# Second transform stages and inverse as 32x32 tiles of the TensorE array

## The chip, the cores and the metric

The kernel runs on one NeuronCore of one Trainium2 chip; the other cores are idle. The metric is the device time of one execution in microseconds (us). The engines are called by their names in the profile: PE (TensorE: matmuls, and PEld, its weight loads), DVE (VectorE), ACT (ScalarE), POOL (GpSimd) and SP (SyncE, used here to issue DMAs). A matmul multiplies a stationary operand (lhsT, loaded as weights) with a moving one (rhs, up to 512 columns) and writes PSUM, which has 8 banks of 512 fp32 columns in each of 128 partitions.

## What is computed

With x = A_q (2048 rows, 512 channels), all in bf16:

```python
xn = layernorm(x)                                  # over the channels
# branch A: a causal shift filter of 4 taps, then a long convolution over the 2048 rows
k_shift[s] = sum over t of k_pad[s + t] * shift_k[3 - t]
kv = k_shift * v
y  = irfft(rfft(kv, 4096) * rfft(ssm_k, 4096))[:2048] + kv * ssm_D
s  = xn * y
# branch B: a gated feed-forward, 512 -> 1792 -> 512
h = gelu(xn @ w_gate) * (xn @ w_up)
g = silu(h @ w_down)
out = x + s * g
```

## The kernel before

**The feed-forward** goes in four quarters of 512 rows. For each quarter, `unit(q, m)` (m = 0 to 13) makes 128 hidden columns: four gate and four up matmuls, a Gelu on ACT (L1149) and a product on DVE (L1152). `down(q)` multiplies back. These matmuls take most of PE's time and need one PSUM bank at a time each (`pF`, at most four banks).

**The long convolution** is a Fourier transform in two stages, done as matmuls, once for the filter ("H", with ssm_D folded in as its first sample) and once for kv ("K"):

- `stage1` (16 tiles of rows each) multiplies with the tables F1, copies the pair of banks out on ACT, and stores to a scratch tensor in HBM (ZH or ZK) whose layout does the reordering between the stages. There are 32 groups of 128 rows in this layout.
- The second stage multiplies each group with `MT[:, 0, :]`, a 128x128 matrix that MSK has made block-diagonal: four blocks of 32x32 on its diagonal, zeros elsewhere. For H, `h_stage2(n)` (n = 0 to 15) does a pair of groups: load BH from ZH, two matmuls (`fwd`), copy out on ACT, store to ZS.
- The spectrum loop at L1063 (n = 0 to 15) does a pair of K groups each: load BK from ZK, two matmuls, multiply with the spectrum HS (two arrays, loaded from ZS by two DMAs, over even and odd partitions), invert, copy out on ACT (BO), store to ZI. The real and imaginary parts lie in even and odd partitions, so the complex product is HB = K x HS[0] plus KS = (K with its even and odd partitions exchanged, and a sign) x HS[1].
- In 14 of the 16 rounds (`psum` true, set by N_SUM = 14) ACT copies K with a sign column (COLS[:, 2:3]) to KB, two DMAs exchange the partitions from KB to KS, DVE multiplies KS by HS[1] and adds it to HB, and the inverse is two matmuls with `MT[:, 1, :]`. In the other two rounds DVE makes KS from PSUM without an exchange, and the inverse adds two matmuls with `MT[:, 2, :]`, a second inverse matrix that contains the exchange.
- At the end BI is loaded from ZI, `y` multiplies with G1, the transposed F1 (32 matmuls), and DVE applies xn and the gate; results are stored as they come.

**The order of the work** on every engine is fixed when the program is built. `Sched` is a list scheduler: each task has an engine, an estimated duration, a priority (the P_... constants; lower goes first), buffers and predecessors; it emits the tasks in the order in which its model starts them. `Trk` puts in the semaphore waits that this order needs. So a task that comes late on the chip holds up what is behind it on its engine. PSUM is one pool of eight banks under two names: `pF` gives single banks from the top, `pC` pairs of banks from the bottom (at most NC_PAIRS = 3 pairs at a time) to the stages of the transform. The DMAs of a stage are issued on SP, those of ZH and ZI on ACT. All matmuls but the transposes are recorded under one line, L634, and all product instructions of the spectrum under L1084, so that groups are told apart by their tiles.

Of the kernel before, what the change touches and what calls it, by code (L numbers as in the profile page):

```python
# [14 lines left out]
DM = 512  # L15
# [13 lines left out]
NC_PAIRS = 3  # L29
SMALL = 1.15 * 262144  # L30
AHEAD = int(4.32)
N_SUM = int(14.8)
HS_FROM = int(13.29)
P_ZS = 0.01
P_HS = 0.2
P_BK = -1
P_KS = -0.49
P_XT = 0.25
P_G1 = 1.22
P_KB = 0.27  # L40
P_PI = 1
P_KM = 3.27
P_LN1 = 2.02
P_LN2 = 3.07
P_LN3 = 7.64
N_HOLD = 3

# [21 lines left out]
class Trk:  # L69
# [112 lines left out]
    def op(self, key, fn, r=(), w=(), accum=False):  # L182
        E = self.engs[key]
        req = self._need(r, w, key, accum)
        with self.nc.body(E["body"]):
            self._do_waits(key, req)
            ins = fn(E["eng"])
            E["seq"] += 1
            v = E["seq"]
            ins.then_inc(E["sem"], 1)  # L190
        sname = E["sem"].name
        self.evid += 1
        snapd = dict(E["wm"])
        snapd[sname] = v
        self.snap[(sname, v)] = snapd
        self._record(r, w, (E["sem"], v, self.evid, key))
        return ins
# [24 lines left out]
class Pool_:  # L222
# [25 lines left out]

    def take(self, i):
        self.used += 1  # L250
        for j in range(i * self.size, (i + 1) * self.size):
            self.busy[j] = True
# [25 lines left out]
class Sched:  # L278


    SLACK = 214.66
# [3 lines left out]
    HEDGE = 1277.99  # L285
# [5 lines left out]
    QUEUE = {"ACT": 1887.67, "DVE": 7268.22}  # L291
    URGENT = 2.78
    DEFER = 11.14
# [49 lines left out]
    def run(self):  # L343
# [5 lines left out]
        while ready:  # L349
            cands = []  # L350
            for t in ready:
# [3 lines left out]
                ok = True  # L355
                for b in t.w:
                    if b.pool is not None and b.slot is None:
                        av = b.pool.find()
                        if av is None:
                            ok = False  # L360
                            break
                        base = max(base, av[0] + self.SEM)
# [60 lines left out]
def build_kernel(nc, A_q, A_k, A_v, A_shift_k, A_ssm_k, A_ssm_D, B_w_gate, B_w_up, B_w_down, out):  # L423
    with ExitStack() as es0:
# [61 lines left out]
        BH = at("BH", [128, 4, 2, DM], BF16, g_at + 8192)  # L486
# [3 lines left out]
        HS = new("HS", [128, 4, 2, 2, DM], BF16)  # L490
# [3 lines left out]
        BK = new("BK", [128, 4, 2, DM], BF16)  # L494
# [6 lines left out]
        ZS = nc.dram_tensor("ZS", [NG // 2, 128, 2, DM], BF16, kind="Internal")  # L501
# [45 lines left out]
        R_cols, R_col1, R_col2 = (res(f"COLS{i}", COLS[:, i:i + 1]) for i in range(3))  # L547
# [27 lines left out]
        R_BH = [res(f"BH{j}", BH[:, j, :, :]) for j in range(4)]  # L575
        R_BK = [res(f"BK{j}", BK[:, j, :, :]) for j in range(4)]
        R_HS = [twins(f"HS{j}", HS[:, j, :, :, :]) for j in range(4)]
        R_KB = [twins(f"KB{j}", KB[:, j, :, :]) for j in range(4)]
        R_KS = [twins(f"KS{j}", KS[:, j, :, :]) for j in range(4)]
# [17 lines left out]
        pBH = Pool_("BH", 4)  # L597
        pBK = Pool_("BK", 4)
        pKB = Pool_("KB", 4)
        pKS = Pool_("KS", 4)  # L600
        pHS = Pool_("HS", 4)
# [271 lines left out]
        def h_transpose(k):  # L873
# [12 lines left out]
            for hf in range(2):  # L886
                def ev(e, h, hf=hf):
# [3 lines left out]
                   rr=lambda hf=hf: R_bank(pp[hf]), ww=R_HTr[8 * hf:8 * hf + 8], prio=1))  # L891
# [20 lines left out]
        bsgn, bphi, bS32, bmsk, bm = B("sgn"), B("phi"), B("s32"), B("msk"), B("m16")  # L912
# [20 lines left out]
        small("DVE", 180.0, lambda h: h.tensor_scalar(COLS[:, 2:3], Q32[:, 10:11], -2.0, 1.0, ALU.mult, ALU.add), [q], [R_col2], [bq[10]], [bsgn])  # L933
# [42 lines left out]
        for t in range(NT):  # L976
            stage1("H", t, HTr[:, t, :], R_HTr[t], [bHTr[k][t // 8] for k in range(KD)], ZH, 1.51)
# [3 lines left out]
        skb = [op([("POOL", 950.0)], lambda e, h, j=j: h.tensor_copy(SKB[:, j, :], SKR[:].rearrange("p (d j) -> p j d", j=4)[:, j, :]), r=[bSKR], w=[bSKB[j]], rr=[R_SKR], ww=[R_SKB[j]], prio=3, after=xnT_tasks + mt_last) for j in (3, 2, 1, 0)]  # L981

        def kshift(i):
# [9 lines left out]
            def rkk(j):  # L993
# [8 lines left out]
               rr=lambda: rkk(3) + [R_SKB[3]], ww=lambda: [R_KAC[a.slot]], prio=4, **af)  # L1002
            for j in (2, 1, 0):
                m = B(f"ktm{i}_{j}", pKTM)
                op([("DVE", dur)], lambda e, h, j=j, m=m: h.tensor_tensor(KTM[:, m.slot, :, :], kk(j), sk(j), ALU.mult), r=need + [bSKB[j], a], w=[m],  # L1005
                   rr=lambda j=j: rkk(j) + [R_SKB[j]], ww=lambda m=m: [R_KTM[m.slot]], prio=4, after=mt_last + sin_tasks + skb)
                op([("DVE", dur)], lambda e, h, m=m: h.tensor_tensor(KAC[:, a.slot, :, :], KAC[:, a.slot, :, :], KTM[:, m.slot, :, :], ALU.add),  # L1007
                   r=[m], w=[a], rr=lambda m=m: [R_KTM[m.slot], R_KAC[a.slot]], ww=lambda: [R_KAC[a.slot]], prio=4)
            kshift_tasks.append(op([("DVE", dur)], lambda e, h: h.tensor_tensor(V[:, t0:t0 + 4, :], KAC[:, a.slot, :, :], V[:, t0:t0 + 4, :], ALU.mult),
               r=[a, bV[i]], w=[bKV[i]], rr=lambda: [R_KAC[a.slot]] + R_V[t0:t0 + 4], ww=R_V[t0:t0 + 4], prio=2.42))  # L1010
# [4 lines left out]
        def z_pair(Z, n):  # L1015
            return bass.AP(Z, 2 * n * 128 * DM, [[DM, 128], [128 * DM, 2], [1, DM]])

        def fwd(p, T, R_T, buf):
            def f(e):
                s = psl(p)  # L1020
                for i in range(2):
                    trk.op("PE", lambda h, i=i: mm(h, ps(s, i), MT[:, 0, :], T[:, buf.slot, i, :], True, True),
                           r=[*R_M, R_T[buf.slot]], w=[R_ps[s][i]], accum=True)
            return f

        d_bh = [dsem(f"d_bh{j}") for j in range(4)]
        h2_tasks = []

        def h_stage2(n):
            bh, p, a = B(f"bh{n}", pBH), B(f"psf{n}", pC), B(f"hf{n}", pAST["K"])  # L1030
            S.add([("SP", ISSUE)], lambda e, n=n, bh=bh: dma(e, BH[:, bh.slot, :, :], z_pair(ZH, n), d_bh[bh.slot], R_Z["H"], [R_BH[bh.slot]]),
                  r=bZ["H"], w=[bh], prio=0.5, nbytes=SMALL, after=zh_tasks)
            h2_tasks.append(S.add([("PE", pe(2))], fwd(p, BH, R_BH, bh), r=[bMT, bh], w=[p], prio=4.26, lat=200.0, heavy="ACT"))
# [269 lines left out]
```

## Time and profile before

| | before |
|---|---|
| time, three runs | 211.63, 211.97, 215.02 us; median 211.97 |
| span of the profiled execution, first to last instruction | 210.6 us (its own time is not given beside the span) |
| PE busy, matmuls | 200.7 us (95%), 992 |
| PEld busy, weight loads | 93.4 us, 992 |
| DVE busy | 171.6 us (81%) |
| ACT busy | 131.7 us (63%) |
| bytes moved by DMA | 61.15 MB, mean 290 GB/s |
| second stage of H (BH with MT) | 32 matmuls, 75.6 to 107.8 us |
| second stage of K (BK with MT) | 32 matmuls, 115.3 to 168.4 us |
| inverse (HB and KS with MT) | 36 matmuls, 119.2 to 177.5 us |
| last stage (BI with G1) | 32 matmuls, 188.9 to 202.7 us |

A row of instructions in the profile reads: line, engine, operation, output <- inputs by their names in the program (numbers left out, so `G` stands for G1 as well), shapes, x count, then the busy time in us and the mean length of one in ns, then the idle time of the engine just before such instructions, and what ended it. Matmuls overlap, so the length of one (379 ns for 512 columns) is not what one more costs. A row of a timeline has the start, the length, engine, line, operation and count of merged instructions. A row of windows has the stretch, its length, and for each engine its busy time and instructions, then PE's granted clock, the DMA engines' busy share and GB/s.

### The profile page before, as it was taken

How to read it: one execution, taken by the hardware profiler on the slowest of the kernel's cores; microseconds unless marked ns; L12 is line 12 of the kernel's file. 1: busy time of each engine (PE TensorE's matmuls, PEld its weight loads, DVE VectorE, ACT ScalarE, POOL GpSimd, SP SyncE). 2: the span in 40 equal slices, each digit the busy share in tenths (PEclk: the TensorE clock that was granted, in tenths of full speed). 3: DMA queues.
4: the chain of work that ended last, by engine and by line, in shares of the span. 5: the costliest groups of instructions: out<-in, count | busy, mean ns of one | idle time of the engine just before them, and what ended most of it. 6: DMA issues, size and time to landing. Idle time of an engine off the chain costs nothing.

```text
span 210.6 us, 2937 instructions
## 1 busy us (share of the span) xinstructions
PE 200.7 (95%) x992; PEld 93.4 (44%) x992; DVE 171.6 (81%) x267; ACT 131.7 (63%) x166; POOL 17.0 (8%) x40
## 2 busy tenths in 40 slices
PE   7789999999997999999999999999999999999993
PEld 2466444444433444444444443344434444444452
DVE  5998878878899898989625969989789797439993
ACT  2478767777962598987953767766747766251021
POOL 7284000030300000000100000000000000000000
PEclk9999999999999999999999999999999999999999
DMA  5999999999999989989899999999999741577951
GB/s 189 350 355 338 371 395 390 401 417 334 143 231 244 211 287 301 355 281 356 241 349 394 262 324 260 372 399 324 304 359 341 260 174 54 167 280 214 329 208 52
DMA packets 48229, 61.15 MB, mean 290 GB/s; under 512 B 13907, under 2 KB 33239, under 8 KB 48214
## 3 DMA queue, kind: packets, MB, share of 16 engines
q1 hardware_dynamic: 41414, 52.44, 78.2%
q10 hardware_dynamic: 6800, 8.52, 11.9%
q8 instruction: 8, 0.13, 0.2%
q14 instruction: 7, 0.06, 0.1%
HBM read 35.78 MB, written 18.87 MB: 260 GB/s over the span
## 4 chain that ended last, share of the span: by engine, by line
PE 56%; DMA 18%; SPq 12%; DVE 7%; ACT 4%; issue 2%; POOL 1%; ACTq 0%; DVEq 0%
PE psall L634 56%; SPq L610 12%; DMA X<-in_A_q_dram 7%; DMA xnT<-XN 6%; DMA HS<-ZS 5%; DVE HB L1084 2%; ACT KB L1101 2%; ACT BO L630 1%; DVE stats L817 1%; DVE G L1178 1%; POOL mv L827 1%; DVE mv L818 0%; DVE XN L830 0%; DVE KS L1084 0%; ACTq L610 0%
## 5 line engine op out<-in xcount | busy, mean ns | idle before, releaser
L634 PE MATMUL psall<-xnT,Wg 128*128 128x512 bf16 (+1 forms) x232 | 54.6, 372 | 3.2 <-ACT xnT L630 1.7
L634 PE MATMUL psall<-xnT,Wu 128*128 128x512 bf16 (+1 forms) x232 | 55.7, 372 | 0.3 <-DVE HB L1084 0.3
L634 PE MATMUL psall<-Wd,HT 128*128 128x512 bf16 (+1 forms) x238 | 54.1, 367 | 0.2 <-DVE G L1178 0.2
L1149 ACT ACTIVATE GE<-psall 128x512 bf16<-128x512 f32 x56 | 33.0, 597 | 29.8 <-PE psall L634 28.5
L1152 DVE TENSOR_TENSOR HT<-psall,GE 128x512 bf16<-128x512 f32 x56 | 37.8, 686 | 15.7 <-PE psall L634 15.6
L634 PEld LDWEIGHTS psall<-xnT,Wg 128*128 128x128 bf16 x232 | 22.3, 98 | 30.0 <-ACT xnT L630 2.3
L634 PEld LDWEIGHTS psall<-Wd,HT 128*128 128x128 bf16 x238 | 23.2, 98 | 25.8 <-DVE G L1178 0.7
L634 PEld LDWEIGHTS psall<-xnT,Wu 128*128 128x128 bf16 x232 | 22.5, 98 | 26.3 <-DVE HB L1084 1.2
L1084 DVE TENSOR_TENSOR HB<-psall,HS 128x1024 bf16<-128x1024 f32 x16 | 19.4, 1219 | 3.4 <-ACT KB L1101 2.3
L630 ACT ACTIVATE BO<-psall 128x1024 bf16<-128x1024 f32 x16 | 16.3, 1022 | 5.4 <-PE psall L634 5.4
L1101 ACT ACTIVATE KB<-psall,COLS 128x1024 bf16<-128x1024 f32 x14 | 15.3, 1112 | 5.9 <-PE psall L634 5.9
L630 ACT ACTIVATE ASH<-psall 128x1024 bf16<-128x1024 f32 x16 | 16.3, 1021 | 4.0 <-PE psall L634 4.0
L1007 DVE TENSOR_TENSOR KAC<-KAC,KTM 128x2048 bf16<-128x2048 bf16 x12 | 14.6, 1220 | 0.2
L1005 DVE TENSOR_TENSOR KTM<-KK,SKB 128x2048 bf16<-128x2048 bf16 x12 | 14.6, 1218 | 0.0
L827 POOL TENSOR_TENSOR mv<-mv,NHALF 128x4 f32<-128x4 f32 (+1 forms) x5 | 7.0, 1399 | 83.8 <-DVE mv L826 83.8
L1178 DVE SCALAR_TENSOR_TENSOR G<-G,psall 128x512 bf16<-128x512 bf16 x12 | 7.9, 683 | 6.0 <-ACT G L1176 5.9
L1184 ACT ACTIVATE G<-psall 128x512 bf16<-128x512 f32 (+1 forms) x5 | 2.6, 511 | 15.8 <-PE psall L634 15.8
L817 DVE BATCH_NORM_STATS2 stats<-X 128x6 f32<-128x512 bf16 x16 | 10.5, 674 | 1.7 <-DMA X<-in_A_q_dram 1.7
L1084 DVE TENSOR_TENSOR KS<-KS,HS 128x1024 bf16<-128x1024 bf16 x14 | 9.5, 682 | 1.8 <-DMA KS<-KB 1.8
L630 ACT ACTIVATE AST<-psall 128x1024 bf16<-128x1024 f32 x11 | 10.6, 1026 | 0.1
L634 PE MATMUL psall<-HB,MT 128*128 128x512 bf16 x32 | 9.9, 381 | 0.7 <-DVE HB L1084 0.6
L1084 DVE TENSOR_TENSOR HB<-HB,KS 128x1024 bf16<-128x1024 bf16 x14 | 9.7, 691 | 0.5
(81 smaller groups left out, 194.1 us busy)
## 6 DMA issues: line engine op xcount, KB each, us to landing
HS<-ZS SPq DMA_DIRECT2D x32, 256.0 KB, 4.9
ZH<-ASH ACTq DMA_DIRECT2D x16, 256.0 KB, 6.6
BH<-ZH SPq DMA_DIRECT2D x16, 256.0 KB, 4.6
BK<-ZK SPq DMA_DIRECT2D x16, 256.0 KB, 5.3
ZI<-BO ACTq DMA_DIRECT2D x16, 256.0 KB, 4.3
BI<-ZI SPq DMA_DIRECT2D x16, 256.0 KB, 4.8
KS<-KB SPq DMA_DIRECT2D x28, 128.0 KB, 4.5
ZK<-AST SPq DMA_DIRECT2D x11, 256.0 KB, 2.9
```

The source lines that it names most:

```text
L610: trk.dma(eng, lambda e: e.dma_start(out=out_ap, in_=in_ap), sem, r=r, w=w)
L630: return h.activation(o, i, ACTF.Copy)
L634: return h.matmul(o, lhsT=l, rhs=r, start=st, stop=sp)
L817: t_stats[t] = op([("DVE", 670.0)], lambda e, h, t=t: h.bn_stats(stats[:, t, :], X[:, t, :]), r=[bX[q][t % 4]], w=[bst[t]], rr=[R_X[t]], w ...
L827: t_pw = op([("POOL", 800.0)], lambda e, hd, ts=ts, n=n: hd.tensor_tensor(mv[:, ts, 3:4], mv[:, ts, 2:3], NHALF[:, 0:n, :], ALU.pow), r=[b ...
L1005: op([("DVE", dur)], lambda e, h, j=j, m=m: h.tensor_tensor(KTM[:, m.slot, :, :], kk(j), sk(j), ALU.mult), r=need + [bSKB[j], a], w=[m], r ...
L1007: op([("DVE", dur)], lambda e, h, m=m: h.tensor_tensor(KAC[:, a.slot, :, :], KAC[:, a.slot, :, :], KTM[:, m.slot, :, :], ALU.add), r=[m], ...
L1084: op([("DVE", dve(1024, rate))], lambda e, h: h.tensor_tensor(o(), i0(), i1(), op_), r=r, w=w, rr=rr, ww=ww, prio=prio)
L1101: op([("ACT", act(1024))], lambda e, h, pk=pk, kb=kb: h.activation(KB[:, kb.slot, :, :].rearrange("p c d -> p (c d)"), ps(psl(pk)), ACTF.C ...
L1149: op([("ACT", act(512))], lambda e, h: h.activation(GE[:, g.slot, :], bank(pg), ACTF.Gelu_apprx_tanh), r=[pg], w=[g], rr=lambda: R_bank(pg ...
L1152: op([("DVE", dve(512, 1))], lambda e, h: h.tensor_tensor(HT[:, q % 2, m, :], bank(pu), GE[:, g.slot, :], ALU.mult), r=[pu, g], w=[bHT[q][m]],
L1178: op([("DVE", dve(512, 1))], lambda e, h, g=g, pc=pc: h.scalar_tensor_tensor(out=g, in0=g, scalar=1.0, in1=pc(), op0=ALU.add, op1=ALU.mult ...
```

## The change

- The second stage takes the four diagonal blocks of MT alone. `tiles` issues, for a unit of four groups, 16 matmuls of a 32x32 stationary block: row block r and column block c of the array, stationary MT[r, k, r], moving the r-th 32 partitions of group c, output on partitions 32c to 32c + 31 of the bank r. So a unit's result comes out with group and row block exchanged, in two pairs of banks. The inverse reads it back in the same way, which restores the order.
- Units of four groups take the place of pairs: eight `h_stage2` and eight `spectrum` units. BH, BK and HS have two buffers of twice the size; BH, BK and HS take half as many DMAs of twice the size. The copies out of PSUM stay at a pair of banks each, two for a unit.
- In all eight spectrum units ACT copies K to KB without a sign, DVE makes both products from KB (HB = KB x HS[0], KS = KB x HS[1]), and the inverse adds two terms with the two matrices MT[1] and MT[2]: 32 tile matmuls. The exchange by DMA, the sum on DVE, the two products from PSUM, N_SUM and the sign column are gone.
- `op` has a `quiet` form, which doesn't increment the engine's semaphore; of a group of tile matmuls only the last one does.
- NC_PAIRS is 4 instead of 3. AHEAD (how many units may be forwarded before an inverse) is 2 units instead of 4 pairs. The scheduler can give a task two pairs at once (`find_all`). Its constants and most priorities have other values, so the order of the whole list is another.

```diff
-NC_PAIRS = 3
+NC_PAIRS = 4
...
-AHEAD = int(4.32)
-N_SUM = int(14.8)
+AHEAD = 2
+T_FWD = 500.0
+T_INV = 760.0
...
-    SLACK = 214.66
+    SLACK = 268.325
...
-    HEDGE = 1277.99
+    HEDGE = 1597.49
...
-    QUEUE = {"ACT": 1887.67, "DVE": 7268.22}
+    QUEUE = {"ACT": 943.835, "DVE": 7268.22}
...
-    DEFER = 11.14
+    DEFER = 40.104
...
+        def tiles(pp, terms):
+
+            todo = [(k, data, rt, row, col) for k, data, rt in terms for row in range(4) for col in range(4)]
+            for n, (k, data, rt, row, col) in enumerate(todo):
+                a, b = slice(32 * row, 32 * row + 32), slice(32 * col, 32 * col + 32)
+                s, i = psl(pp[row // 2]), row % 2
+                trk.op("PE", lambda h: h.matmul(ps(s, i)[b, :], lhsT=MT[a, k, a], rhs=data(col)[a, :], start=n < 16, stop=n >= len(todo) - 16, tile_position=(32 * row, 32 * col)),
+                       r=[*R_M, *rt], w=[R_ps[s][i]], accum=True, quiet=n < len(todo) - 1)
...
-        for n in range(16):
+        for n in range(8):
             h_stage2(n)
...
+            S.add([("PE", T_FWD)], fwd(pk, BK, R_BK, bk), r=[bMT, bk], w=pk, prio=P_K2, lat=200.0, after=t_inv[n - AHEAD:n - AHEAD + 1] if n >= AHEAD else [])
+            for h in range(2):
+                op([("ACT", act(1024))], lambda e, hd, h=h: copy(e, hd, flat(KB, kb[h]), ps(psl(pk[h]))),
+                   r=[pk[h]], w=[kb[h]], rr=lambda h=h: R_ps[psl(pk[h])], ww=lambda h=h: [R_KB[kb[h].slot]], prio=P_KB)
+                for k, o, T, R_o in ((0, hb[h], HB, R_HB), (1, ks[h], KS, R_KS)):
+                    op([("DVE", dve(1024, 2))], lambda e, hd, h=h, k=k, o=o, T=T: hd.tensor_tensor(flat(T, o), flat(KB, kb[h]), flat(HS, hs, (k, 2 * h)), ALU.mult),
+                       r=[kb[h], hs], w=[o], rr=lambda h=h: [R_KB[kb[h].slot]] + R_HS[hs.slot], ww=lambda o=o, R_o=R_o: [R_o[o.slot]], prio=P_MUL)
+
+            def inv(e):
+                tiles(pi, [(m, lambda c, T=T, bb=bb: T[:, bb[c // 2].slot, c % 2, :], [R_b[b.slot] for b in bb]) for m, T, R_b, bb in ((1, HB, R_HB, hb), (2, KS, R_KS, ks))])
+            t_inv.append(S.add([("PE", T_INV)], inv, r=[bMT, *hb, *ks], w=pi, prio=P_PI, lat=200.0))
```

## The prediction

> **What bounds the kernel.** I read the page's busy times and slices first, then the windows by stage, then the chain, then the groups that the change touches.
>
> ```profile
> span 210.6 us, 2937 instructions
> PE 200.7 (95%) x992; PEld 93.4 (44%) x992; DVE 171.6 (81%) x267; ACT 131.7 (63%) x166; POOL 17.0 (8%) x40
> PE   7789999999997999999999999999999999999993
> ...
> PEclk9999999999999999999999999999999999999999
> ```
>
> PE (the matmul engine) is busy in all slices but the head, one dip and the tail, always at the full clock. The page warns that a busy PE is not PE at its peak, so I looked at how matmuls follow each other. In the timeline:
>
> ```profile
> 27.60 1.03 PE L634 MATMUL psall<-xnT,Wu 128*128 128x512 bf16 x4
> ...
> 30.19 1.89 PE L634 MATMUL psall<-xnT,Wg 128*128 128x512 bf16 x8
> ```
>
> Four take 1.03 us and eight 1.89, so one more costs (1.89-1.03)/4 = 0.215 us (0.2157 from longer rows), whereas one alone lasts 379 ns; 379 - 216 = 163 ns is the filling and emptying that the next matmul normally hides. PE is truly streaming, back to back. The windows by stage say where it is not:
>
> ```profile
> 0.00:60.00 60.00, 56.39 (x318) 28.70 (x318) 50.12 (x105) 42.15 (x51) 15.97 (x39) 1.00 1.04 329
> 60.00:115.00 55.00, 53.52 (x248) 24.11 (x248) 44.74 (x61) 39.10 (x50) 1.01 (x1) 1.00 0.96 298
> 115.00:180.00 65.00, 63.48 (x290) 27.12 (x288) 56.08 (x74) 43.63 (x54) 0.00 (x0) 1.00 0.85 284
> 180.00:210.60 30.60, 27.26 (x141) 13.50 (x138) 20.60 (x30) 6.83 (x11) 0.00 (x0) 1.00 0.63 214
> ```
>
> The second number is the length, the third PE busy. PE idles 3.6 us at the start, 1.5 near 60 to 65, 1.5 in 115 to 180, and 3.3 at the end, 9.9 in all. So the end is set by the amount of matmul work: what is taken off PE between 60 and 207 us comes off the time, as long as the work that remains can be fed.
>
> **What comes off PE.** The rows of the groups (count, then busy and mean):
>
> ```profile
> L634 PE MATMUL psall<-BH,MT 128*128 128x512 bf16 x32 | 9.2, 379 | 0.0
> L634 PE MATMUL psall<-BK,MT 128*128 128x512 bf16 x32 | 9.2, 380 | 0.2
> L634 PE MATMUL psall<-HB,MT 128*128 128x512 bf16 x32 | 9.9, 381 | 0.7 <-DVE HB L1084 0.6
> L634 PE MATMUL psall<-KS,MT 128*128 128x512 bf16 x4 | 1.5, 379 | 0.0
> ```
>
> These 100 matmuls go: 100 x 0.2157 = 21.6 us of stream time (their busy sums count the overlap twice).
>
> **What comes onto PE.** Eight forward units for h and eight for k of 16 tile matmuls each, and eight inverse units of 32: 24 groups, 32 rounds of sixteen, 512 tile matmuls, each still streaming 512 columns. The trace holds no tile matmul, so I bound a round. Below: sixteen at once in the time of one stream, 0.216 us, 32 x 0.2157 = 6.9 us in all, net -14.7. Above: the nearest row for weight load plus matmul when the stream is short is the transposes:
>
> ```profile
> 12.64 1.16 PE L882 MATMUL psall<-ident,Hn 128*128 128x128 bf16 x16
> ```
>
> Sixteen pairs in 1.16 us with a single one at 226 ns: (1.16-0.23)/15 = 62 ns a pair. If a tile pair costs as much, 512 x 0.062 = 31.7 us. That is an upper price, since 128 columns at 0.2157/512 per column already stream for 54 of those 62 ns. To either I add that a group may neither overlap the matmul before nor the one after: 2 x 163 ns x 24 = 7.8 us (bounds 0 and 7.8). I take the stream price with the full filling and emptying, because the group stands between whole-array matmuls with another use of the array on either side: forward 0.326 + 0.216 = 0.54 us, inverse 0.76, so 16 x 0.54 + 8 x 0.76 = 14.7 us. **Net on PE: 14.7 - 21.6 = -6.9 us**; bounds -14.7 and 31.7 + 7.8 - 21.6 = +17.9. The diff tells its planner 500 and 760 ns for these; that only orders the list and is no measurement.
>
> A rule of the Trainium skill speaks against the change: "TensorE: Matmul & The Clock Gate", Part 3 (The mechanism), has weight loads overlap running matmuls only where the row group differs, and the new loop puts four tiles of the same row group one after another. In this trace whole-array loads, which cover all row groups, overlap running matmuls every time:
>
> ```profile
> 76.67 0.31 PEld L634 LDWEIGHTS psall<-BH,MT 128*128 128x128 bf16 x2
> ...
> 76.89 0.59 PE L634 MATMUL psall<-BH,MT 128*128 128x512 bf16 x2
> ```
>
> The first load runs under the matmuls before it and the second under the first of these two, so the row contradicts the rule as it is worded, and I do not price by it. By the rule at its worst nothing runs at once and 512 x 0.2157 = 110 us replace 21.6. The same part's model, one matmul plus about 4 ns for each further tile, would make a forward group 379 + 60 = 0.44 us, an estimate from that page, and the sum some 1 to 2 us better than mine.
>
> **DVE, ACT, DMA.** DVE loses 16 products read from PSUM (1219 ns), 14 sums (691), 14 products (682) and two at 1220: 19.5 + 9.7 + 9.5 + 2.4 = 41.1 us; it gains 32 products of two SBUF operands at 0.682 = 21.8. Net -19.3 us, priced at 0: the work that sets the end is PE's stream, and in 115 to 180 DVE already has 8.9 us to spare. Were PE not the bound, those 19 us would be the gain. ACT trades 14 scaled copies (1.11) for 16 plain ones (1.02): +0.8 us, hidden, since ACT is 63% busy. The sign column costs DVE 0.15 us early, nothing. SP loses 28 swap issues (596 ns) and 16 HS issues (597), and 8 each of BH and BK (0.37 and 0.57): some 34 us of queue; the swaps' 28 x 128 KB leave the DMA. Zero too: SP's longest waits are for PE results (25.7 us), so it follows PE.
>
> The spectrum's latency changes shape. Now a block pair goes PSUM -> sign copy 1.11 -> two swap issues and 4.5 us of landing -> 0.68 -> 0.69 -> inverse. After, a unit of four blocks goes two copies (2.04, in turn) and then the second half's two products (1.36) -> inverse, 3.4 us with no DMA in it. The inverse waits for both halves, but nothing on PE has to follow at once: the next gate and up matmuls stand in the list. Behind a unit's copies on ACT queue the Gelus, whose banks PE refills; one copy delays them 1.02 us as now.
>
> **The new order and the PSUM claim.** A unit claims four banks at once, twice over (forward and inverse); with four pairs allowed these cover all eight banks that the four gate and up banks share. I bound what the order does by PE's waits between 60 and 200 us:
>
> ```profile
> PE psall L634 <- DVE G L1178: 1.3, 2, 1.1
> PE psall L634 <- DVE HB L1084: 0.9, 2, 0.6
> PE psall L634 <- DMA xnT<-XN: 0.4, 1, 0.4
> ```
>
> All gone: -2.6. Each of eight spectrum units paying one wait as long as the longest: +8.8. I take 0, nearest to what stands there with pairs twice as frequent. The end keeps its 3.3 us after PE, the ACT, DVE and output DMA of the last rows. It also has room: from the last inverse (177.3) to PE's end come 29.4 us of matmuls, and the path copy 1.0, ZI 4.5, BI 4.8, y 32 x 0.216 = 6.9 needs 17.
>
> **Sum.** 0 for the rest, -6.9 on PE: the span goes from 210.6 to 203.7. The page gives no time beside the span; the median of the three runs is 211.97, so 1.4 us lie around it, and I predict 203.7 + 1.4 = 205.1, 3.2% less. A change of this kernel under about 2% can hardly be told from none, by its three times.
>
> **Rivals.**
> 1. *Pairs issue too slowly (slower).* Place: inside the 24 groups. PE must load 512 small weights instead of 100 large ones. With filling paid, break-even is (21.6-7.8)/512 = 27 ns a pair; above that it loses. At 62 ns the time is 212 + 17.9 = 229.9; at 35, 216, which is where over 2% begins. For: nothing here shows pairs closer than 62. Against: 54 of those 62 are streaming. 0.12.
> 2. *Given back as waits.* Units of four blocks hold the banks: 0.9 us lost at each of eight units, near the longest wait above, makes +7, so 212. For: near 60 to 65 PE did stand for banks held by late DVE work. Against: DVE is 19 us lighter. 0.14.
> 3. *The tiles don't run at once*: 16 x 0.216 a round, 212 + 88.8 = 301. Against: the overlapping loads above. 0.02.
> 4. *Groups overlap their neighbours fully*: -14.7, 197.3. For: ordinary matmuls with new weights do. 0.06.
>
> My forecast holds the other 0.66, with its own range 201 to 207.7: on one side the groups' filling and emptying half hidden (-3.9), on the other three tenths of the waits' upper bound (0.3 x 8.8 = 2.6). The range for 8 in 10 reaches from 199 past the waits' case into the low end of rival 1: 199 to 214. Faster 0.72 (forecast and rival 4), same 0.14, slower 0.14 (rivals 1 and 3).
>
> **What would show it.** Tile matmuls whose starts lie 14 ns apart or less within a round, and forward groups occupying 0.45 to 0.6 us from the matmul before to the one after; PE busy near 194; DVE near 152; no KS swaps; PE's waits in 60 to 200 still under 4 us. I am wrong if a round takes over 0.45 us, if PE's idle time grows beyond 14 us, or if the head before 60 us moves by more than 2.

## The result

The changed kernel takes 206.93 us (median of four executions, 204.16 to 207.24), the kernel before, run four times too, 212.11 (211.63 to 215.02). The ratio, taken over the fast executions of both, is 0.969 with the 95% interval 0.960 to 0.978: faster by 3.1%, or 6.5 us of 212.11. The two medians alone differ by 5.2 us (2.4%), the two profiled spans by 5.6; all three lie within that interval. Forecast were 205.1 us and 3.2%.

The page of the changed kernel's profiled execution, whose own time was 206.78:

```profile
span 205.0 us, 3648 instructions
...
PE 191.1 (93%) x1404; PEld 86.2 (42%) x1404; DVE 153.1 (75%) x252; ACT 130.9 (64%) x168; POOL 17.0 (8%) x40
...
PE   7588999999989999999999999999978999999990
...
PEclk9999999999999999999999999999999999999997
```

PE is busy 9.6 us less, and the span is only 5.6 us shorter: PE's idle time went from 9.9 to 205.0 - 191.1 = 13.9. The windows by stage (stretch, length, then busy time and instructions of PE, PEld, DVE, ACT, POOL, PE's granted clock, DMA share, GB/s) say where:

```profile
0.00:60.00 60.00, 54.02 (x310) 27.64 (x311) 51.28 (x105) 39.54 (x48) 15.96 (x39) 1.00 1.04 333
60.00:115.00 55.00, 55.00 (x353) 23.67 (x351) 46.01 (x62) 40.21 (x54) 1.01 (x1) 1.00 0.83 271
115.00:180.00 65.00, 62.42 (x640) 24.80 (x639) 38.06 (x61) 47.76 (x63) 0.00 (x0) 1.00 0.79 261
180.00:205.00 25.00, 19.65 (x105) 10.09 (x103) 17.74 (x26) 3.39 (x6) 0.00 (x0) 0.94 0.67 227
```

PE now idles 6.0 us in the head (3.6 before), nothing from 60 to 115 (1.5), 2.6 from 115 to 180 (1.5), and 5.35 at the end (3.3); from 180 us to its last matmul it does not idle. DVE is lighter by 18 us between 115 and 180: 38.1 busy, 56.1 before.

The groups of tile matmuls (count, then busy and mean ns of one, then idle before):

```profile
L1067 PE MATMUL psall<-BK,MT 32*32 32x512 bf16 x128 | 3.9, 385 | 1.5 <-DVE G L1201 1.5
...
L1067 PE MATMUL psall<-BH,MT 32*32 32x512 bf16 x128 | 3.5, 385 | 0.0
L1067 PE MATMUL psall<-HB,MT 32*32 32x512 bf16 x128 | 3.5, 385 | 0.0
L1067 PE MATMUL psall<-KS,MT 32*32 32x512 bf16 x128 | 3.4, 375 | 0.1
```

128 of them, at 385 ns each, are busy for 3.5 us in eight units: 0.44 us a round (0.43 in the timeline below). So all sixteen of a round run at once. What a group occupies on PE is read from its neighbours, in the timeline of PE around one forward group (start, length, matmuls merged):

```profile
75.55 1.89 PE L678 MATMUL psall<-xnT,Wu 128*128 128x512 bf16 x8
77.37 0.43 PE L1067 MATMUL psall<-BH,MT 32*32 32x512 bf16 x16
77.74 1.04 PE L678 MATMUL psall<-xnT,Wg 128*128 128x512 bf16 x4
```

and around one inverse group:

```profile
121.75 1.89 PE L678 MATMUL psall<-xnT,Wg 128*128 128x512 bf16 x8
123.57 0.43 PE L1067 MATMUL psall<-HB,MT 32*32 32x512 bf16 x16
123.80 0.42 PE L1067 MATMUL psall<-KS,MT 32*32 32x512 bf16 x16
124.15 1.68 PE L678 MATMUL psall<-xnT,Wu 128*128 128x512 bf16 x7
```

Sixteen starts lie within 0.43 - 0.385 = 0.045 us, 3 ns apart. The last of the eight ordinary matmuls starts 7 x 0.2157 = 1.51 us after the first, so at 77.06; without a group the next would start 0.216 later. It starts at 77.74: the forward group occupies 0.68 - 0.216 = 0.46 us. For the inverse, 124.15 - 123.26 - 0.216 = 0.67 us. The second round costs 0.21, one stream; entering and leaving the tiles costs 0.25 us for each group. In the trace 13 of the 16 forward groups and 7 of the 8 inverse groups show these same prices; the others have a wait in them. All groups together: 16 x 0.46 + 8 x 0.67 = 12.7 us in place of 21.6.

The longest wait of PE between 60 and 200 us, and its neighbours in the list of waits:

```profile
PE psall L1067 <- DVE G L1201: 1.5, 1, 1.5
PE psall L678 <- ACT GE L1172: 0.4, 1, 0.4
PE psall L678 <- DVE HT L1175: 0.3, 1, 0.3
```

The timeline of all engines there:

```profile
152.23 0.69 DVE L1134 TENSOR_TENSOR HB<-KB,HS 128x1024 bf16<-128x1024 bf16 x1 [3.87 <-DMA HS<-ZS]
...
152.84 1.28 DVE L1201 SCALAR_TENSOR_TENSOR G<-G,psall 128x512 bf16<-128x512 bf16 x2
...
154.17 0.44 PE L1067 MATMUL psall<-BK,MT 32*32 32x512 bf16 x16 [1.52 <-DVE G L1201]
```

This is the new kind of wait. DVE stands for 3.87 us at a product whose HS load has not landed; behind it in DVE's order are two gate multiplications that read PSUM; PE's next forward group needs those banks. DVE is 75% busy and still holds PE up.

What grew at the end is DVE's part. The last matmuls and the last work of DVE, before and after:

```profile
202.96 4.30 PE L634 MATMUL psall<-Wd,HT 128*128 128x512 bf16 x33
208.03 0.29 DVE L1187 TENSOR_TENSOR G<-G,X 128x256 bf16<-128x256 bf16 x1
```

```profile
197.96 1.69 PE L678 MATMUL psall<-Wd,HT 128*128 128x256 bf16 x14
202.21 0.29 DVE L1210 TENSOR_TENSOR G<-G,X 128x256 bf16<-128x256 bf16 x1
```

From PE's end to DVE's end it was 1.1 us and is 2.85, in which DVE does not pause; the output DMAs after it take 2.3 and 2.5 us.

### The profile page after: what moved, and what is told of

Its sections match the earlier page's. It is cut to its first block, busy times and chain, and to the rows that moved or that the text cites. A ratio compares the mean times of both kernels' runs of the same rounds, so it can differ in the third digit from the quotient of the medians.

```text
span 205.0 us, 3648 instructions
## 1 busy us (share of the span) xinstructions
PE 191.1 (93%) x1404; PEld 86.2 (42%) x1404; DVE 153.1 (75%) x252; ACT 130.9 (64%) x168; POOL 17.0 (8%) x40
## 4 chain that ended last, share of the span: by engine, by line
PE 75%; DVE 10%; ACT 7%; DMA 5%; POOL 1%; issue 1%; ACTq 0%
PE psall L678 71%; PE psall L1067 5%; DMA ZI<-BO 3%; DMA X<-in_A_q_dram 2%; DVE stats L861 1%; DVE G L1255 1%; DVE XN L1255 1%; POOL mv L871 1%; ACT F L768 1%; ACT BO L674 1%; DVE HT L1175 1%; DVE XN L874 1%; DVE G L1210 1%; DVE G L1209 1%; DVE G L1267 1%
## 5 line engine op out<-in xcount | busy, mean ns | idle before, releaser
L678 PE MATMUL psall<-Wd,HT 128*128 128x512 bf16 (+1 forms) x238 | 53.0, 367 | 0.0
L678 PEld LDWEIGHTS psall<-Wd,HT 128*128 128x128 bf16 x238 | 22.7, 98 | 25.8 <-issue 1.8
L678 PEld LDWEIGHTS psall<-xnT,Wu 128*128 128x128 bf16 x232 | 21.2, 98 | 27.5 <-issue 2.0
L1134 DVE TENSOR_TENSOR HB<-KB,HS 128x1024 bf16<-128x1024 bf16 x16 | 11.0, 685 | 10.8 <-DMA HS<-ZS 6.6
L674 ACT ACTIVATE KB<-psall 128x1024 bf16<-128x1024 f32 x16 | 15.4, 1023 | 2.1 <-PE psall L1067 1.1
L674 ACT ACTIVATE AST<-psall 128x1024 bf16<-128x1024 f32 x11 | 10.7, 1026 | 1.3 <-DMA ZS<-AST 0.7
L861 DVE BATCH_NORM_STATS2 stats<-X 128x6 f32<-128x512 bf16 x16 | 10.5, 673 | 1.3 <-DMA X<-in_A_q_dram 1.3
L1201 DVE SCALAR_TENSOR_TENSOR G<-G,psall 128x512 bf16<-128x512 bf16 x12 | 8.0, 684 | 4.1 <-ACT G L1199 3.9
L1134 DVE TENSOR_TENSOR KS<-KB,HS 128x1024 bf16<-128x1024 bf16 x16 | 11.0, 685 | 0.0
L1255 DVE SCALAR_TENSOR_TENSOR G<-psall,G 128x1024 bf16<-128x1024 f32 x6 | 7.3, 1224 | 4.4 <-PE psall L678 4.4
L1083 ACT ACTIVATE AST<-psall 128x1024 bf16<-128x1024 f32 x9 | 8.8, 1022 | 1.1 <-PE psall L1067 1.0
```

Of the source, the lines that this page charges most:

```text
L674: return h.activation(o, i, ACTF.Copy)
L678: return h.matmul(o, lhsT=l, rhs=r, start=st, stop=sp)
L861: t_stats[t] = op([("DVE", 670.0)], lambda e, h, t=t: h.bn_stats(stats[:, t, :], X[:, t, :]), r=[bX[q][t % 4]], w=[bst[t]], rr=[R_X[t]], w ...
L1083: op([("ACT", act(1024))], lambda e, hd, p=p, a=a: hd.activation(ast["K"][a.slot].rearrange("p c d -> p (c d)"), ps(psl(p)), ACTF.Copy, sc ...
L1134: op([("DVE", dve(1024, 2))], lambda e, hd, h=h, k=k, o=o, T=T: hd.tensor_tensor(flat(T, o), flat(KB, kb[h]), flat(HS, hs, (k, 2 * h)), AL ...
L1255: op([("DVE", dve(1024, 1))], lambda e, h, p=p, g=g, f=1.0 if j < 6 else 2.0: h.scalar_tensor_tensor(out=g, in0=ps(psl(p)), scalar=f, in1= ...
```

## The experiments

Each kernel is the changed one with one edit (e9 with two), with a profile of one execution, and timed beside the kernel before on the same chip: four executions, ten of e6, e8 and e9. The kernel before took 212.1 to 213.4 us on these chips, so I compare ratios. "Cost" is the difference of the ratio to the changed kernel's 0.969, times 212.11; the interval of the changed kernel alone makes that uncertain by 1.9 us. By the quotients of the medians the losses would be 0.6 to 1.5 us smaller.

| run | us | ratio to before, 95% | cost, us |
|---|---|---|---|
| changed kernel | 206.93 | 0.969 (0.960 to 0.978) | 0 |
| e1 whole-array matmuls | 218.66 | 1.024 (1.019 to 1.029) | +11.7 |
| e2 tile loops exchanged | 205.32 | 0.964 (0.957 to 0.970) | -1.2 |
| e3 every tile signals | 205.67 | 0.967 (0.960 to 0.973) | -0.6 |
| e4 both products twice | 216.66 | 1.016 (1.012 to 1.021) | +9.9 |
| e11 HB product twice | 208.54 | 0.981 (0.977 to 0.984) | +2.4 |
| e12 exchange DMAs back | 217.54 | 1.020 (1.014 to 1.026) | +10.7 |
| e10 half of the HS loads | 204.58 | 0.961 (0.957 to 0.964) | -1.8 |
| e5 the old order's constants | 217.14 | 1.016 (1.008 to 1.024) | +9.9 |
| e6 HS in half buffers | 214.37 | 1.004 (1.001 to 1.008) | +7.5 |
| e7 last stage copied by ACT | 206.59 | 0.969 (0.963 to 0.975) | 0.0 |
| e8 planner told measured costs | 212.56 | 0.995 (0.992 to 0.999) | +5.5 |
| e9 e8 and e7 together | 212.10 | 0.995 (0.992 to 0.999) | +5.5 |

**Only the tiles undone (e1).** The same units, buffers, products and order; each group becomes 128x128 matmuls with the block-diagonal MT.

```diff
-            todo = [(k, data, rt, row, col) for k, data, rt in terms for row in range(4) for col in range(4)]
+            todo = [(j, k, data, rt, c) for j, (k, data, rt) in enumerate(terms) for c in range(4)]
...
-                trk.op("PE", lambda h: h.matmul(ps(s, i)[b, :], lhsT=MT[a, k, a], rhs=data(col)[a, :], start=n < 16, stop=n >= len(todo) - 16, tile_position=(32 * row, 32 * col)),
+                trk.op("PE", lambda h: mm(h, ps(s, i), MT[:, k, :], data(c), j == 0, j == len(terms) - 1),
```

> The changed kernel with its list of work untouched, but every group of tile matmuls replaced by whole-array matmuls with the 128x128 matrix: 4 forward and 8 inverse per unit instead of 16 and 32 tiles. In the changed kernel's trace a forward group takes 0.46 us of PE from the start that would have been next to the start that is, an inverse group 0.67, together 12.7 us; whole-array they take 16 x 0.863 + 8 x 1.726 = 27.6. Theory (the gain is PE's stream): PE busy rises by 14 to 15 us and the time by 11 to 15, to 218 to 222, well above the kernel before, since this version also has the second inverse matrix in all rounds. Rival (the gain is the lighter DVE and the missing exchange by DMA, PE is not the limit): the time rises by under 5 us and stays below 212.

```profile
PE 204.5 (94%) x1004; PEld 97.0 (45%) x1020; DVE 154.1 (71%) x252; ACT 132.1 (61%) x168; POOL 16.9 (8%) x40
```

PE is busy 13.4 us longer than with tiles, the span 12.0 (217.0), and the time costs 11.7: PE's stream goes nearly one to one into the time. The step from the kernel before to this one is told by the same price. It has 128 whole-array matmuls where the kernel before had 100, since the second inverse matrix is now used in every unit: 28 x 0.2157 = 6.0 us more, and it is 1.0244 x 212.11 - 212.11 = 5.2 us slower. DVE's 17.5 us less (171.6 to 154.1), the exchange DMAs gone and the new order together bring, net, no more than the 0.8 us between the two, less than the 1 us that e1's interval leaves open. That is a net only: a gain of one of them and a loss of another would not show in it. So, in this list, the change is +5 us in its restructuring and -12 in its tiles.

**The order of the tiles (e2).** Consecutive tiles now lie in different row groups.

```diff
-            todo = [(k, data, rt, row, col) for k, data, rt in terms for row in range(4) for col in range(4)]
+            todo = [(k, data, rt, row, col) for k, data, rt in terms for col in range(4) for row in range(4)]
```

> The changed kernel with the two loops over tiles exchanged: consecutive tile matmuls now lie in different row groups of the array instead of in the same one. Theory (weight loads overlap whatever the row group): starts within a round stay 3 ns apart, a forward group at 0.46 us, the time within 0.5% of the changed kernel's. Rival (the rule that loads overlap only between different row groups): a group gets shorter by 0.1 us or more, the time by 2 us or more.

```profile
119.47 0.43 PE L1067 MATMUL psall<-BK,MT 32*32 32x512 bf16 x16
119.84 1.04 PE L678 MATMUL psall<-xnT,Wu 128*128 128x512 bf16 x4
...
124.73 0.43 PE L1067 MATMUL psall<-HB,MT 32*32 32x512 bf16 x16
124.96 0.42 PE L1067 MATMUL psall<-KS,MT 32*32 32x512 bf16 x16
125.31 1.04 PE L678 MATMUL psall<-xnT,Wu 128*128 128x512 bf16 x4
```

The same lengths and the same 0.37 and 0.58 us to the next ordinary matmul. The sixteen weight loads of a round take 0.14 us in either order. The rule by row groups that the prediction weighed (the Trainium skill, "TensorE: Matmul & The Clock Gate", Part 3, The mechanism) is not seen in this kernel.

**Every tile signals (e3).** The `quiet` form is not used.

```diff
-                       r=[*R_M, *rt], w=[R_ps[s][i]], accum=True, quiet=n < len(todo) - 1)
+                       r=[*R_M, *rt], w=[R_ps[s][i]], accum=True)
```

> The changed kernel with every tile matmul incrementing PE's semaphore, not only the last of a group. Theory (each completion is passed on while the array works on): ordinary matmuls all signal and follow each other at 0.216 us, so nothing in this trace prices it; if the signals of sixteen tiles that end together are passed on one by one at 20 to 30 ns, a forward group's result is released some 0.4 us later and an inverse's 0.4 to 0.8, but PE's stream need not wait: the time rises by 0 to 3 us. Rival (the next matmul waits for the signals too): 16 x 0.4 + 8 x 0.8 = 12.8 us on PE, time about 219.

PE busy 189.8 us, the same groups, no cost in the time. One forward group and the copy behind it:

```profile
120.09 0.43 PE L1067 MATMUL psall<-BK,MT 32*32 32x512 bf16 x16
...
120.75 1.94 ACT L674 ACTIVATE KB<-psall 128x1024 bf16<-128x1024 f32 x2 [0.26 <-PE psall L1067]
```

ACT starts 0.23 us after the group's end, where 0.11 is the least in the changed kernel. But this is not the price of fifteen more signals. With every tile signalling, the first copy waits for the eight tiles of its own pair of banks alone, no longer for the whole group. The events of PE's semaphore in e3's trace come one by one, 34 ns apart, from 0.40 us after the group's start: the eighth at 120.73, just before the copy, the sixteenth at 121.00, 0.48 us after the group's end. The one signal of the changed kernel comes 0.09 us after it. So the whole group is signalled 0.39 us later, as the expectation had it, and behind an inverse, with 32 signals, the first copy starts 0.56 us after the group's end (0.11 in the changed kernel). The time does not show it: PE's next matmuls start when they did, and the second copy has to wait for the first on ACT anyway.

**DVE's relief given back (e4, e11).** All 32 products of the spectrum are issued twice (e4, 21.9 us of DVE), or, with `range(2 - k)` in the edit, the 16 for HB only (e11, 11 us). The lists of PE, ACT and SP stay as they are.

```diff
+                        for _ in range(2):
+                            trk.op(e, lambda hd: hd.tensor_tensor(flat(T, o), flat(KB, kb[h]), flat(HS, hs, (k, 2 * h)), ALU.mult), r=[R_KB[kb[h].slot]] + R_HS[hs.slot], w=[R_o[o.slot]])
```

> The changed kernel with each of the 32 spectrum products on DVE made twice (same result, same place in the list): +32 x 0.685 = 21.9 us of DVE work between 120 and 169 us, which brings DVE's total to 175 us, near the 171.6 of the kernel before. Theory of the prediction (DVE's relief is worth nothing, PE's stream hides it): the time rises by at most 2 us. Rival (PE keeps streaming only because DVE became lighter; the spectrum's chain sets when the last stage can start): the time rises by 5 to 15 us, and the first matmul of the last stage comes later by as much.

> The changed kernel with only the 16 products HB made twice: +11 us on DVE instead of the +21.9 that cost 10 us. Theory A (DVE has slack and then has none: before the change it had 8.9 us to spare in 115 to 180, now 27): the first 11 us are nearly free, under 2 us, and the second 11 cost the rest. Theory B (every DVE microsecond in a unit lies on the unit's chain): half of the 10, 4 to 6 us, and the last inverse comes as much later.

The windows of 115 to 180 us, of e4:

```profile
115.00:180.00 65.00, 53.72 (x588) 20.43 (x579) 55.69 (x87) 42.77 (x54) 0.00 (x0) 1.00 0.76 238
```

and of e11:

```profile
115.00:180.00 65.00, 60.48 (x625) 23.77 (x627) 47.59 (x75) 46.97 (x60) 0.00 (x0) 1.00 0.79 257
```

In e4 DVE is as busy there (55.7) as it was in the kernel before (56.1), and PE loses 8.7 us of the 62.4 that it did in this stretch. Its waits in e4, between 60 and 210 us:

```profile
PE psall L1067 <- DVE KS L1136: 4.2, 4, 1.6
PE psall L1067 <- DVE HT L1177: 3.4, 4, 1.3
PE psall L1067 <- DVE G L1203: 1.1, 1, 1.1
```

The first 11 us on DVE cost 2.4, the next 11 cost 7.5: there is slack first, and then none (the first step is hardly above the uncertainty). For e4 the prediction's theory, that DVE's relief is worth nothing, is refuted. PE does not wait for DVE as a whole but for single late products, and for banks that DVE has not read. The kernel before carried the same DVE load in this stretch with 1.5 us of idle PE, in pairs and in another order, so the 9.9 us are the price with this list, not with every list.

**The exchange back as traffic (e12).** After each of the first 14 KB copies SP issues the two exchange DMAs again, to a tensor that nobody reads; nothing waits for their landing.

```diff
+                    if 2 * n + h < 14:
+                        for g in range(2):
+                            dma("SP", ZX[2 * n + h][g::2, :, :], KB[1 - g::2, kb[h].slot, :, :], d_zx[(2 * n + h) % 4][g], [R_KB[kb[h].slot]], [R_zx[2 * n + h][g]])
```

> The changed kernel with the exchange by DMA put back as traffic: 28 DMAs of 128 KB on SP, each with exchanged partitions as before, from KB to a scratch tensor in HBM that nothing reads; lists of PE, DVE and ACT unchanged, SP waits for each KB copy before it issues. Theory of the prediction (the exchange's DMAs were hidden, removing them is worth nothing): within 1 us. Rival (queue time on SP and bytes on the DMA engines delay HS and BK): the last inverse comes 2 to 6 us later and the time rises by as much.

The timeline of e12:

```profile
133.25 1.98 SPq L654 DMA_DIRECT2D ZX<-KB  x2
...
136.74 0.69 DVE L1141 TENSOR_TENSOR HB<-KB,HS 128x1024 bf16<-128x1024 bf16 x1 [8.55 <-DMA HS<-ZS]
...
138.69 1.89 PE L678 MATMUL psall<-xnT,Wg 128*128 128x512 bf16 x4 [6.10 <-DVE HT L1182]
```

It is the chain of the changed kernel's one wait, made long. HS loads stand behind the exchange issues, which wait for KB copies and share the DMA engines; DVE waits 8.55 us for HS, the feed-forward's product HT stands behind it, and PE waits 6.10 us for HT. The windows of e12 add a second price:

```profile
132.00:139.00 7.00, 0.90 (x4) 0.23 (x3) 2.26 (x4) 1.02 (x1) 0.00 (x0) 0.83 1.03 387
139.00:144.00 5.00, 4.78 (x43) 1.45 (x43) 2.03 (x4) 1.19 (x2) 0.00 (x0) 0.56 0.86 318
144.00:150.00 6.00, 5.84 (x56) 2.44 (x56) 2.86 (x5) 4.00 (x5) 0.00 (x0) 1.00 0.73 252
```

and a second wait of PE, in the timeline, with a window just behind it:

```profile
163.54 0.44 PE L1067 MATMUL psall<-BK,MT 32*32 32x512 bf16 x16 [3.45 <-DVE G L1208]
```

```profile
164.00:165.00 1.00, 1.00 (x3) 0.34 (x4) 1.00 (x3) 0.92 (x1) 0.00 (x0) 0.50 0.98 382
```

After the first stall PE ran for about 5 us at a granted clock of 0.56 on average (0.50 up to 143.4 us), its ordinary matmuls some 0.43 us apart, before the clock was back at 1.00. The second wait, 3.45 us for a bank that DVE had not read, was followed by 3.4 us at 0.50 (163.9 to 167.3). Together these are 4.7 + 3.4 us of work at half the clock, so an estimated 4 of the 10.5 us that the span grew. The cost is above what either theory expected. How the rest divides between the queue, the traffic and the place where I put the issues, which the planner did not know of, this run does not tell.

**Half of the HS loads (e10).** After the first load of each HS buffer, the loads of the odd partitions are left out, so the products use old values there: six DMAs and 3.1 MB less.

```diff
-                for h in range(2):
+                for h in range(1 if hs.slot in seen else 2):
```

> The changed kernel without the loads of HS into odd partitions, except the first one into each of the two buffers: 6 of 16 HS DMAs and 3.1 MB less, so from the third unit on the odd partitions hold the spectrum of an earlier unit (this part of the computation is left out); PE's, DVE's and ACT's lists stay. The spectrum's loads and stores are 2 MB a unit, 16.8 MB in the 51 us from 118 to 169, at a DMA busy share of 0.9 to 1.04 up to 160 us. Theory (DMA sets the pace of the units): the last inverse comes 2 to 8 us earlier than 168.7, PE's idle time there vanishes, the time falls by 2 to 4 us, held by PE. Rival (the pace is the list's, PE reaches the groups when the list says): the last inverse moves by under 1.5 us, time within 1 us of the changed kernel's.

The 1.5 us wait behind G L1201 is gone, PE is busy 63.45 of the 65 us in 115 to 180 (62.42 with all loads), and the last inverse starts 1.7 us earlier. That agrees with a late HS load as the cause of this wait, but one profile does not show it: with all loads the same wait is 1.5 us in the changed kernel, 0.4 in e2 and absent in e3, whose last inverse starts 2.0 us earlier than the changed kernel's. DVE's waits for HS differ as well: 6.6, 2.8 and 4.7 us in these three, 2.6 in e10. So the lateness varies from one profiled execution to another. The gain in time, 1.8 us, is at the edge of the uncertainty and between the two expectations.

**The old order (e5).** All of the planner's constants and priorities that still exist get the values of the kernel before; tiles and units stay.

```diff
-    SLACK = 268.325
+    SLACK = 214.66
...
-P_K2 = 6.56
+P_K2 = 5.9
```

> The changed kernel with the scheduler's constants and priorities of the kernel before (NC_PAIRS stays 4; what has no counterpart before keeps its value), so the same instructions in an order that was not fitted to them. Theory (the gain is in the instructions, the order only keeps PE fed): PE busy stays at 191, its idle time grows, and the time is 1 to 6 us above the changed kernel, 207 to 212. Rival (the new order is where the gain comes from): the time is back at the kernel before or above, 212 or more.

The rival's number came: the whole gain is gone. The profiled execution was the longest of the four (span 219.4); PE is idle for 23.7 us of it. Its longest waits between 60 and 220 us:

```profile
PE psall L678 <- DVE V L1052: 4.2, 1, 4.2
PE psall L1067 <- ACT BO L674: 2.8, 1, 2.8
```

The longest ends at 65.8 us, before any tile matmul, at the work on V that makes kv; after it, and again from 158.4 us, the granted clock is 0.50 for 3.4 us. So part of this cost has nothing to do with the tiles. What the tiles are worth in this order no run shows: that would need whole-array groups in the same order.

**True costs for the planner (e8).** It is told what the groups were measured to occupy.

```diff
-T_FWD = 500.0
-T_INV = 760.0
+T_FWD = 460.0
+T_INV = 675.0
```

> The changed kernel with the planner's costs for a forward and an inverse group set to what the trace shows, 460 and 675 ns instead of 500 and 760; the instructions are the same, the order follows anew. Theory (the list is good where its costs are right): 0 to 1 us less. Rival (the other constants were fitted around the old costs, so any new order is a little worse): 0 to 3 us more.

The rival is right again: the truer model gave a worse list, by 5.5 us. The timeline of PE in e8 at its end:

```profile
177.53 12.29 PE L678 MATMUL psall<-Wd,HT 128*128 128x512 bf16 x70
189.66 4.72 PE L678 MATMUL psall<-BI,G 128*128 128x512 bf16 x20
195.88 1.17 PE L678 MATMUL psall<-BI,G 128*128 128x512 bf16 x4 [1.51 <-DMA BI<-ZI]
```

The list puts 70 matmuls of the feed-forward ahead of the last stage, which starts at 189.7 (184.3 in the changed kernel), and then has nothing else left to cover BI's loads. In 115 to 180 us PE idles for only 0.1 us in e8 (2.6 in the changed kernel), yet the last inverse starts at 176.9 us instead of 168.6, with 102 matmuls behind it instead of 154. So the waits of the changed kernel are gone, and the time is lost at the end: 2.3 us of waits for BI, 3.4 us at a granted clock of 0.50 from 197.8 us, and 8.0 us from PE's end to the span's, 5.3 in the changed kernel.

**HS in four half buffers (e6).** So that a load can start after half a unit; the list follows anew.

```diff
-pHS = Pool_("HS", 2)
+pHS = Pool_("HS", 4)
```

> The changed kernel with the HS buffers as four halves of a unit instead of two whole units, so that a half is loaded again as soon as its two products are done, and after only its own half of ZS is stored. In the changed kernel's trace DVE waits 3.9 us for HS near 148 to 152 and PE stands 1.5 us for a bank that DVE should have freed. Theory (the doubled unit of the loads made this wait): DVE's waits for HS go from 6.6 to under 3 us, PE's idle time in 115 to 180 from 2.6 to about 1, the time falls by 1 to 2 us. Rival (the loads are late because the DMA queues are full, not for their buffers): no change, or longer by the smaller transfers.

A miss, 7.5 us worse: the first matmul of the last stage moved to 193.4. DVE no longer waits for HS at all between 115 and 180 us (6.6 us before the edit), as the theory had it, but what that is worth can't be told from the loss by the new list; in the time this run says only what e8 says.

**The tail (e7, e9).** ACT, nearly idle there, copies the last stage out of PSUM in place of DVE's reading it; e7 with the changed kernel's lists of PE and SP, e9 with those of e8.

```diff
+            yb = B(f"yb{j}", pKB)
+            op([("ACT", act(1024))], lambda e, h, p=p, yb=yb, f=1.0 if j < 6 else 2.0: h.activation(KB[:, yb.slot, :, :].rearrange("p c d -> p (c d)"), ps(psl(p)), ACTF.Copy, scale=f), r=[p], w=[yb],
...
+            op([("DVE", dve(1024, 2))], lambda e, h, yb=yb, g=g: h.tensor_tensor(g, KB[:, yb.slot, :, :].rearrange("p c d -> p (c d)"), g, ALU.mult), r=[yb, *([bGX[j]] if j < 6 else [])], w=[bS[j], *([] if j < 6 else bXN[ts])],
```

> The changed kernel with the last stage's results copied out of PSUM by ACT (1.02 us each, ACT is nearly idle there), so that DVE multiplies two bf16 operands in SBUF, 0.69 us instead of 1.22, eight times; PE's and SP's lists are the same. In the changed kernel DVE works without a pause from 193 to 202.5, while PE ends at 199.65. Theory (the time after PE's last matmul grew from 3.3 to 5.4 us because DVE is behind): DVE's stretch is 8 x 0.53 = 4.3 us shorter, what follows PE's end falls to 3.5 to 4 us, the time by 1.3 to 2 us. Rival (the tail is the output DMAs or PE): no change, or up to 1 us longer by the extra step on ACT.

> Both edits of the two runs before together: the list planned with the measured group costs (460 and 675 ns), and the last stage's results copied out of PSUM by ACT; PE's and SP's lists are those of the run with measured costs alone. With those costs alone the first matmul of the last stage came at 189.7 and the span ended 20.1 us later, with PE idle and DVE at work without a pause: from there DVE has 8 x (1.22 + 0.69) + 5 x 0.85 = 19.5 us to do. Theory (where that first matmul comes late, DVE's work on the last stage sets the end): DVE's part shrinks by 8 x 0.53 = 4.3 us and the time by 3 to 4.5, from 212.6 to 208 to 209.6, though the same edit gave nothing in the fitted list, where PE was busy nearly to the end. Rival (the slow list is slow for other reasons, such as loads of BI that land late): under 1.5 us.

DVE is 4.0 us lighter in e7 (149.1), yet 5.0 us still follow PE's last matmul, 5.3 before the edit: DVE now waits for ACT's copies (1.4, 1.0 and 0.5 us between 188 and 197 us) and works without a pause only from 198.5 to its end at 202.9. In e9 PE's longest wait, from its timeline, is for a load:

```profile
200.39 2.98 PE L678 MATMUL psall<-BI,G 128*128 128x512 bf16 x6 [2.41 <-DMA BI<-ZI]
```

The gains that my theory forecast came in neither. That does not refute that DVE holds the tail, since the edit puts a copy of 1.02 us ahead of each product while it takes 0.53 off; what bounds the tail stays open.

**What ties them together.** In the nine profiles that share PE's list (the changed kernel, e1, e2, e3, e4, e7, e10, e11, e12) the time from the start of the last KS matmul to the end of the span is always 35.8 to 36.1 us: 168.9 to 205.0 in the changed kernel, 181.0 to 217.0 in e1, 179.1 to 215.2 in e4, 179.4 to 215.5 in e12. From the last inverse on, the list streams as written. What these kernels differ by is how soon the last inverse comes. No version that computes everything is clearly faster than the changed kernel.

## Why the prediction was right, step by step

- **The bound** was PE's stream, as said. e1 shows it: 13.4 us more of PE, 12.0 more of span.
- **PE's groups** were priced too high. Forecast were 0.54 and 0.76 us and 14.7 in all; measured were 0.46, 0.67 and 12.7. The mis-sized term is the filling and emptying: 0.25 us for a group, not the 0.33 of two full ones. So the net is -8.9 in place of -6.9. With -0.85 for the warm-up matmuls at the start (11 took 4.88 us before and 4.03 after, no work saved: the trace has the full clock from 6.2 us on before and from 4.2 after, so the prediction's "always at the full clock" does not hold for the start) that makes -9.75; the busy time shows -9.6. The Trainium skill's model, which the prediction set beside its own (0.44 us for a forward group, an estimate from the page), was the nearer one: the span of a round, which it models, measures 0.43, and the group occupies 0.46. By that model the sum would have been 24 x 0.1 = 2.4 us lower, not the 1 to 2 that the prediction says.
- **PE's idle time** was to stay at 9.9; it is 13.9. This is the step that failed, though not where the prediction looked: the waits that it priced at 0 (between -2.6 and +8.8), those between 60 and 180, came to -0.4, so rival 2, waits at every unit, did not come. The two ends, which it kept as they were, grew: the head by 2.4 us (about 0.85 of them is the warm-up, 0.96 a wait for a Gelu near 18 us), the tail by 2.0, of which DVE's last work is 1.8. The forecast total came out right since 2.9 us more off PE's busy time met 4.0 us more of idle; that the two errors nearly cancel is luck. Of the three signs that were to show me wrong, one came, the head moving by 2.4 us, over the 2, and two nearly, the idle time just under 14 us and a round at 0.43 to 0.44 us, under the 0.45.
- **DVE's relief at 0** agrees with the step from the kernel before to e1: with 17.5 us less on DVE, nothing beyond 0.8 us came, net of the new order. What the relief is worth in the old order no run shows. As a condition the 0 was incomplete. The new list uses up the room: e4 and e11 show that giving 11 us back costs 2.4 and giving 22 back costs 9.9. "DVE has 8.9 us to spare" was a mean over 65 us, and PE waits for single products.
- **The exchange at 0**, "since SP follows PE", has the same gap. e12 shows that in this order DMAs ahead of HS loads cost up to 10.7 us, by way of DVE, the banks and the clock. What the exchange cost in the old order, no run tells.
- **The order at 0** was the weakest step. e5, e8 and e6 change the list alone or with little else, and cost 5.5 to 9.9 us, most of what the tiles bring. The argument by room, 29.4 us of matmuls behind the last inverse against a path of 17, held in the changed kernel's list, which keeps 30.4 us there and does not idle in them. In e8's list 19.0 us are left, still more than 17, and PE waits: the argument leaves out the DVE work of the last rows, and that BI's later loads stand on SP behind waits for PE's matmuls and DVE's results (6.2 us each in e8).
- **Rival 1** (slow pairs, break-even at 27 ns) fell with 3 ns between starts; rival 3 with it. **Rival 4** (197.3, full overlap) fell since each group pays 0.25 us. Of the small terms, the KS swaps are gone, DVE at 153.1 was forecast near 152, and ACT fell by 0.8 where it was to rise by 0.8.

Open is why executions of one and the same changed kernel spread by 3 us (spans 202.4 to 205.4; the wait behind the late HS load, 1.5 us in the changed kernel's profile and absent in e3's, fits a part of it), and what a list fitted to the true costs by search, in place of one given two new numbers, would bring.

## What to carry to other kernels

Small block-diagonal matmuls can be packed on the array at the price of about one stream for sixteen, plus 0.25 us for each group that stands between whole-array matmuls; so make the groups as long as the data allow. Where the order is written ahead, a saving on the bounding engine can be lost again by the list, as e5, e6 and e8 show, and each engine that "has room" must be asked what stands behind its latest operand: in-order DVE behind one late load stopped PE by way of PSUM banks. Change one part at a time, but read the prices with care: here whole-array groups, double products, the exchange as traffic and the old constants each cost 10 to 12 us alone, where the whole gain is 6.5. Such prices hold in the changed kernel's list and do not add up to the gain.

## What the runs showed of the hardware that I had not expected

- Sixteen tile matmuls of 512 columns start 3 ns apart, and their weight loads all within 0.14 us, in either order of the loops. By contrast an ordinary matmul follows after 216 ns.
- Signals of tiles that end together come one by one, 34 ns apart in e3: the last of sixteen 0.48 us after the group's end, a single one after 0.09. They hold up the readers of the result, not PE's next matmuls; here that cost nothing in the time.
- A stall of PE can cost more than itself. After 6.10 us of idle PE in e12, some 5 us passed at a granted clock of 0.56, about 2.2 us of work lost (5 x 0.44, an estimate); after 3.45 us of idle it was 0.50 for 3.4 us. The Trainium skill, "TensorE: Matmul & The Clock Gate", Part 1 (The HAM clock gate), has the clock fall to half after an idle window of about 3.4 us and come back after as long a busy one; this run agrees in kind. None of the changed kernel's waits between 60 and 200 us, 1.5 us at most, lowered its clock of 1.00.
